# One multiplication per unit moved from VectorE to GpSimd, with a new order of work, in a fused recurrence and rational-activation kernel

## The chip, the cores and the metric

The kernel runs on one core of one Trainium2 chip. The metric is device time in microseconds (us). Before the change, three runs gave a median of 220.79 us, with 219.61 as the lowest and 221.04 as the highest.

A core has several engines that run side by side, each taking its own instructions strictly in order: PE (TensorE, matmuls), DVE (VectorE), ACT (ScalarE) and POOL (GpSimd). SP (SyncE) issues only DMAs here. POOL both computes and issues DMAs, and it can do that only in the order of its one queue.

## The reference

The first half is a gated linear recurrence over 768 positions, for 4 batches with 8 heads of 48 features. Its result, laid out as 3072 tokens of 384 features, goes into a two-layer block with a rational activation.

```python
f = 1.0 / (1.0 + np.exp(-f_logit))
for t in range(S):                       # S = 768
    state = f[:, :, t, :, None] * state + einsum('bhd,bhe->bhde', k[:, :, t], v[:, :, t])
    y[:, :, t] = einsum('bhd,bhde->bhe', q[:, :, t], state)

h = x @ w_in                             # 3072x384 @ 384x2048
P = a[0] + a[1]*h + a[2]*h**2 + a[3]*h**3
Q = 1.0 + abs(b[0])*abs(h) + abs(b[1])*h**2
out = (P / (Q + 1e-06)) @ w_out          # 3072x2048 @ 2048x384
```

## The kernel before

**Units.** The work is cut into 12 units. A unit is 256 positions of one batch, all heads at once; units 0 to 3 are the first 256 positions of the four batches, 4 to 7 the next, 8 to 11 the last. A unit's later batch-mate needs the state that the earlier one leaves.

**The recurrence part of a unit.** ACT makes the log of the forget gate (`ef`, `ls`, L190 and L195). PE sums it along positions with triangular matrices (`cs`, L205). ACT takes the exponential twice (`A n 0` and `A n 1`, L221): a decay factor for q and its inverse for k, each 128 partitions by 768 in float32. DVE multiplies the loaded q and k by them (`xa n 0` for q, `xa n 1` for k, L227), writing bf16. PE transposes both products (`T`, L239), and ACT copies the transposes out of PSUM (`Te`, L249). PE forms the scores (`sc`, L264); DVE masks them, reading PSUM (`mk`, two per unit, L272). PE adds up the output (`yi`, `yb`, L286), and ACT brings it to SBUF (`ye`, tile `xT`, L349). In between PE builds the new state (`kv`, `si`, tile `sv`), and DVE scales it, again reading PSUM (`st`, L359). GpSimd makes a small rearranged copy of v for each unit (`vm`, two per unit, L279).

**The block part of a unit.** PE multiplies `xT` by w_in, in four quarters of the hidden 2048 (`h`, tile `hp`, L368); ACT casts each quarter to bf16 (`hy`, L382). With this bf16 `hy`, DVE makes the square (`sq`, L386, tile `h`), the absolute value (`ab`, L394, tile `z`), and the numerator by steps `p1` (L428), `p2` (L433), `pm` (L442). Two sums of two tiles are needed, and each can be made in different ways:

- The denominator, square plus absolute value. PE can add both in PSUM by identity matmuls (`u`, L402, then `ln`, L407, as the logarithm on ACT). DVE can add them (`zv`, L412), or a DMA issued by POOL can accumulate (`zd`, L416); for these two, `lz` (L420) is the logarithm.
- The numerator's last sum, either by an accumulating DMA from POOL (`ta`, L446) or by DVE (`tv`, L450).

ACT then takes the exponential of the negative logarithm (`ex`, L424), DVE multiplies it on (`gm`, L454), and PE multiplies by w_out (`o`, L462). ACT copies the result out (`oe`, L469), and a DMA stores it.

**The order.** A string `ORDER` lists every step of all units. A loop at the end goes through it and issues each step; nothing is reordered afterwards, so the string sets the order on each engine and on each DMA queue. Numbers such as `8 16` are the sixteenths of the hidden dimension that a step covers, so `8 16` is one half of a unit and `4 8` a quarter. `@2` names one of four PSUM slots. `dz k` is k filler matmuls on PE. Loads of f, k and q are issued by SP, loads of v and of the weights by POOL. One piece of w_in is held back by a wait on the step `ls 1`, through a helper `behind` that makes an instruction wait until an earlier marked step has finished.

Of the kernel before, what the change touches and what calls it, by code (L numbers as in the profile page):

```python
# [29 lines left out]
def kernel(  # L30
# [12 lines left out]
    nc = tc.nc  # L43
# [3 lines left out]
    HP = H // 2  # L47
# [14 lines left out]
    ld = ctx.enter_context(tc.tile_pool(name="ld", bufs=3))  # L62
# [30 lines left out]
    marks = {}  # L93

    def unit(n):
        if n not in units:
            c, b = divmod(n, B)
            units[n] = dict(c=c, b=b, qk=qkp[n % 2], ls=lsp[n % 2], vm=vmp[n % 2], st=states[b])
        return units[n]

    def slot(i, shape, dtype, name):
        return slots[i].tile(shape, dtype, name=name, tag="s")
# [114 lines left out]
    def A(n, x, a0=0, a1=HP):  # L217
        s = unit(n)
        t = A_sb[:, :, x, 2 * D * a0:2 * D * a1]
        src = s["cs", a0][:, :, 0:2 * D * (a1 - a0)]  # L220
        nc.scalar.activation(t, src, AF.Exp, scale=1.0 if x else -1.0)  # L221

    def xa(n, x, *args):
        s = unit(n)
        a0, a1 = args or (0, HP)
        hh = slice(2 * a0, 2 * a1)
        return nc.vector.tensor_mul(  # L227
            s["qk"][:, :, x, hh, 0:D],
            s["qk"[x]][:, hh].rearrange("p h i d -> p i h d"),
            A_sb[:, :, x].rearrange("p i (h d) -> p i h d", h=H)[:, :, hh])  # L230

    def T(n, *args):
        s = unit(n)
        a0, a1, sl = args if len(args) == 3 else (0, HP, args[0])
        t = s["tp", a0] = slot(sl, [P, 2, 2, HP, P], BF16, "tp")
        for x in (1, 0):
            for i in range(2):
                for p in range(a0, a1):
                    nc.tensor.transpose(t[:, x, i, p, :],  # L239
                                        s["qk"][:, i, x, 2 * p:2 * p + 2, :].rearrange("t h d -> t (h d)"), ident)  # L240

    def Te(n, *args):
        a0, a1 = [x for x in args if x != "s"] or (0, HP)
        s = unit(n)
        if "T" not in s:
            s["T"] = at.tile([P, 2, 2, HP, P], BF16, name="qkT")
        d, t = s["T"][:, :, :, a0:a1], s["tp", a0][:, :, :, a0:a1]
        if "s" in args:
            return nc.scalar.copy(d.bitcast(F32).rearrange("p x i a t -> p (x i) (a t)"),  # L249
                                  t.bitcast(F32).rearrange("p x i a t -> p (x i) (a t)"))  # L250
        return nc.vector.tensor_copy(d.rearrange("p x i a t -> p (x i) (a t)"),
                                     t.rearrange("p x i a t -> p (x i) (a t)"))
# [224 lines left out]
    def behind(i, mark):  # L477
        tc.add_manual_dep(i.ins, marks[mark].ins.name,
                          mybir.DependencyInfo(mybir.DependencyClass.Sync, mybir.DependencyReason.DATA),
                          reason="begins behind it")  # L480

    steps = dict(ld=load, wi=load_w_in, wo=load_w_out, ab_=load_ab, cu=const_u, ci=const_i, cm=const_m,
                 cz=const_z, fa=coef_a, fb=coef_b, fr=coef_r, ef=ef, ls=ls, cs=cs, A=A, xa=xa, T=T, Te=Te,
                 sc=sc, mk=mk, vm=vm, yi=yi, yb=yb, kv=kv, si=si, ye=ye, ae=ae, st=st, h=h, hy=hy, sq=sq, ab=ab, u=u, ln=ln,
                 zv=zv, zd=zd, sa=sa, lz=lz, ex=ex, p1=p1, p2=p2, pm=pm, ta=ta, tv=tv, gm=gm, o=o, oe=oe, so=store, dz=dz)
    for step in ORDER.replace("\n", ";").split(";"):
        if step.strip():
            name, *args = step.split()
            marks[".".join([name] + [x for x in args if x.isdigit()])] = steps[name](
                *(int(x.lstrip("@")) if x.lstrip("@").isdigit() else x for x in args))  # L490


# [1 line left out]
_INS = ['q', 'k', 'v', 'f_logit', 'moe_w_in', 'moe_w_out', 'moe_a', 'moe_b']  # L494
_OUTS = [((3072, 384), 'float32')]


# [23 lines left out]
```

## Time and profile before

| | us |
|---|---|
| median of three runs | 220.79 |
| the profiled execution's own time | 220.24 |
| its span, first to last instruction | 218.4 |
| PE busy in the span | 204.7 |
| DVE busy in the span | 203.2 |
| ACT busy in the span | 199.9 |
| POOL busy in the span | 92.0 |

The span is 1.84 us shorter than the time of its execution; that remainder lies around the instructions. The busy time of PE contains modelled ends of overlapping matmuls, and a POOL instruction's busy time contains its stalls, so these two rows are rougher than those of DVE and ACT. The granted TensorE clock was at full speed for the whole span.

### The profile page before, as it was taken

How to read it: one execution, taken by the hardware profiler on the slowest of the kernel's cores; microseconds unless marked ns; L12 is line 12 of the kernel's file. 1: busy time of each engine (PE TensorE's matmuls, PEld its weight loads, DVE VectorE, ACT ScalarE, POOL GpSimd, SP SyncE). 2: the span in 40 equal slices, each digit the busy share in tenths (PEclk: the TensorE clock that was granted, in tenths of full speed). 3: DMA queues.
4: the chain of work that ended last, by engine and by line, in shares of the span. 5: the costliest groups of instructions: out<-in, count | busy, mean ns of one | idle time of the engine just before them, and what ended most of it. 6: DMA issues, size and time to landing. Idle time of an engine off the chain costs nothing.

```text
span 218.4 us, 7180 instructions
## 1 busy us (share of the span) xinstructions
PE 204.7 (94%) x3178; PEld 140.8 (64%) x3178; DVE 203.2 (93%) x247; ACT 199.9 (92%) x209; POOL 92.0 (42%) x91
## 2 busy tenths in 40 slices
PE   6999989889799999999999999999999999999992
PEld 2456758548477658657758658668668568686551
DVE  3577999999999999999999999999999999999991
ACT  4733999999999999999999999999999999999990
POOL 5250055969145901113953304954232526433300
PEclk9999999999999999999999999999999999999999
DMA  5999999999598999956999996999889794999853
GB/s 137 246 225 206 217 248 220 211 233 247 64 214 164 227 214 283 179 101 179 195 232 204 222 255 169 174 237 221 162 161 227 144 158 77 170 192 189 157 215 144
DMA packets 60911, 42.15 MB, mean 193 GB/s; under 512 B 51152, under 2 KB 54992, under 8 KB 60880
## 3 DMA queue, kind: packets, MB, share of 16 engines
q0 software_dynamic: 21232, 22.81, 65.4%
q1 hardware_dynamic: 39360, 18.68, 33.4%
q8 instruction: 25, 0.41, 0.8%
q10 hardware_dynamic: 288, 0.20, 0.3%
q14 instruction: 6, 0.05, 0.1%
HBM read 25.17 MB, written 4.72 MB: 137 GB/s over the span
## 4 chain that ended last, share of the span: by engine, by line
ACT 36%; DVE 31%; PE 21%; issue 5%; DMA 5%; SPq 0%; DVEq 0%; ACTq 0%
ACT qi L424 9%; ACT hy L382 9%; PE op L462 9%; PE hp L368 6%; ACT lq L420 5%; DVE scm L272 4%; DVE h L386 4%; DVE gall L454 4%; DVE qkp L227 4%; DVE gall L442 3%; DMA z<-h 3%; ACT A L221 3%; DVE gall L428 3%; DVE z L394 3%; DMA fn<-in_f_logit_dram 2%
## 5 line engine op out<-in xcount | busy, mean ns | idle before, releaser
L462 PE MATMUL op<-w_out_sb,gall 128*128 128x384 bf16 x384 | 70.1, 327 | 0.4 <-ACT hy L382 0.4
L368 PE MATMUL hp<-xT,w_in_sb 128*128 128x256 bf16 x576 | 66.6, 273 | 1.1 <-ACT xT L349 0.8
L368 PEld LDWEIGHTS <-w_in_sb 128*128 128x128 bf16 x576 | 56.0, 98 | 11.4 <-issue 2.8
L279 POOL COPY vmp<-vn 128x128 bf16<-128x128 bf16 x24 | 43.9, 1841 | 30.1 <-DMA vn<-in_v_dram 26.1
L462 PEld LDWEIGHTS <-gall 128*128 128x128 bf16 x384 | 35.4, 98 | 23.8 <-DVE gall L454 0.9
L382 ACT CAST hy<-hp 128x1024 bf16<-128x1024 f32 x48 | 47.2, 1068 | 2.3 <-PE hp L368 2.3
L424 ACT ACTIVATE qi<-lq 128x2048 bf16<-128x2048 f32 (+1 forms) x26 | 46.8, 1838 | 0.0
L420 ACT ACTIVATE lq<-z 128x2048 f32<-128x2048 bf16 (+1 forms) x20 | 36.9, 1847 | 0.6 <-DMA z<-h 0.6
L446 POOL DMA_DIRECT2D gall<-hy x17 | 14.8, 925 | 50.6 <-PE hp L368 18.4
L416 POOL DMA_DIRECT2D z<-h x18 | 17.6, 1081 | 30.3 <-issue 10.5
L454 DVE TENSOR_TENSOR gall<-gall,qi 128x2048 bf16<-128x2048 bf16 (+1 forms) x26 | 29.6, 1144 | 0.3 <-ACT qi L424 0.2
L442 DVE TENSOR_TENSOR gall<-gall,h 128x2048 bf16<-128x2048 bf16 (+1 forms) x26 | 29.4, 1143 | 0.0
L386 DVE TENSOR_TENSOR h<-hy 128x2048 bf16<-128x2048 bf16 (+1 forms) x26 | 27.4, 1063 | 2.1 <-ACT hy L382 2.1
L272 DVE TENSOR_TENSOR scm<-sc,mask 128x1024 bf16<-128x1024 f32 x24 | 28.4, 1218 | 0.0
L221 ACT ACTIVATE A<-cs 128x768 f32<-128x768 f32 (+1 forms) x26 | 19.5, 813 | 0.8 <-DVE qkp L227 0.8
L394 DVE TENSOR_SCALAR z<-hy 128x2048 uint16<-128x2048 uint16 (+1 forms) x28 | 17.4, 629 | 0.2 <-ACT hy L382 0.2
L428 DVE TENSOR_SCALAR gall<-hy,a_sb 128x4096 bf16<-128x4096 bf16 (+1 forms) x14 | 17.2, 1231 | 0.0
L433 DVE TENSOR_SCALAR hy<-hy,a_sb 128x4096 bf16<-128x4096 bf16 (+1 forms) x14 | 16.7, 1192 | 0.0
L114 POOL DMA_DIRECT2D vn<-in_v_dram x12 | 14.0, 1166 | 1.6 <-PE y L286 1.6
L349 ACT ACTIVATE xT<-y 128x768 bf16<-128x768 f32 x12 | 10.3, 858 | 4.1 <-PE y L286 4.1
L227 DVE TENSOR_TENSOR qkp<-kn,A 128x768 bf16<-128x768 f32 (+1 forms) x13 | 11.6, 893 | 2.1 <-ACT A L221 2.1
L239 PE MATMUL tp<-ident,qkp 128*128 128x128 bf16 x192 | 12.9, 219 | 0.2
(70 smaller groups left out, 262.1 us busy)
## 6 DMA issues: line engine op xcount, KB each, us to landing
gall<-hy POOLq DMA_DIRECT2D x16, 512.0 KB, 6.5
z<-h POOLq DMA_DIRECT2D x15, 512.0 KB, 7.3
fn<-in_f_logit_dram SPq DMA_DIRECT2D x11, 384.0 KB, 8.6
kn<-in_k_dram SPq DMA_DIRECT2D x11, 384.0 KB, 8.9
qn<-in_q_dram SPq DMA_DIRECT2D x11, 384.0 KB, 7.6
out_dram<-osb SPq DMA_DIRECT2D x11, 384.0 KB, 4.2
vn<-in_v_dram POOLq DMA_DIRECT2D x12, 192.0 KB, 7.7
w_in_sb<-in_moe_w_in_dram POOLq DMA_DIRECT2D x4, 384.0 KB, 9.9
```

What stands on the lines that cost most here:

```text
L221: nc.scalar.activation(t, src, AF.Exp, scale=1.0 if x else -1.0)
L272: return nc.vector.tensor_mul(t, s["sc", g].rearrange("s r a i t -> s (r a) (i t)"), mb)
L279: nc.gpsimd.tensor_copy(s["vm"][:, :, :, 32 * x:32 * x + 16], src)
L368: nc.tensor.matmul(t[:, m - m0, :], w_in_sb[:, kk, m * P:(m + 1) * P], s["x"][:, kk].rearrange("p i j t -> p (i j t)"), start=(kk == 0), s ...
L382: nc.scalar.copy(fl(big(s, "hy", "hy", 3), m0, m1), fl(s["hp", m0], 0, m1 - m0))
L386: return nc.vector.tensor_mul(fl(big(s, "h2", "h2", 2), m0, m1), fl(s["hy"], m0, m1), fl(s["hy"], m0, m1))
L394: return nc.vector.tensor_scalar(fl(big(s, "z", "z", 2), m0, m1).bitcast(U16), fl(s["hy"], m0, m1).bitcast(U16), 0x7FFF, None, op0=ALU.bit ...
L420: nc.scalar.activation(fl(lq, m0, m1), fl(s["z"], m0, m1), AF.Ln, scale=regs[2], bias=1.0 + 1e-6)
L424: nc.scalar.activation(fl(qi, m0, m1), fl(lq, m0, m1), AF.Exp, scale=-1.0)
L442: return nc.vector.tensor_mul(fl(s["g"], m0, m1), fl(s["g"], m0, m1), fl(s["h2"], m0, m1))
L454: return nc.vector.tensor_mul(fl(s["g"], m0, m1), fl(s["g"], m0, m1), fl(qi, m0, m1))
L462: nc.tensor.matmul(s["op"][:, j, 0:DM], s["g"][:, m, P * j:P * j + P], w_out_sb[:, m, :], start=(s["on", j] == 1), stop=(s["on", j] == KF))
```

## The change

Four things change in the code:

- `xa` takes a mark `p`. With it, the multiplication runs on GpSimd and not on VectorE, and it waits until the last "wide" step listed ahead of it has finished. Wide steps are `sq`, `ab`, `p1`, `p2`, `pm`, `gm`, `zv` and `tv`: DVE's steps on bf16 tiles in SBUF.
- From unit 3 to unit 11, the k product (`xa n 1`) carries this mark: nine of twelve. All q products stay on DVE.
- The ways of the two sums are drawn anew. Identity sums by PE (`u` with `ln`) go from 11 quarters to 2. DVE's `zv` goes from 2 halves to 6 halves and 4 quarters. DMA's `zd` goes from 15 halves and 3 quarters to 14 halves and 2 quarters, `ta` from 16 halves and 1 quarter to 17 halves and 2 quarters, and DVE's `tv` from 6 halves and 3 quarters to 5 halves and 2 quarters.
- `ORDER` is a new list. All other steps occur as often as before, with 39 filler matmuls where there were 38.

```diff
     def xa(n, x, *args):
         s = unit(n)
-        a0, a1 = args or (0, HP)
+        pool = "p" in args
+        a0, a1 = [y for y in args if y != "p"] or (0, HP)
         hh = slice(2 * a0, 2 * a1)
-        return nc.vector.tensor_mul(
+        i = (nc.gpsimd if pool else nc.vector).tensor_mul(
             s["qk"][:, :, x, hh, 0:D],
             s["qk"[x]][:, hh].rearrange("p h i d -> p i h d"),
             A_sb[:, :, x].rearrange("p i (h d) -> p i h d", h=H)[:, :, hh])
+        if pool:
+            behind(i, "wide")
+        return i
...
     for step in ORDER.replace("\n", ";").split(";"):
...
-            marks[".".join([name] + [x for x in args if x.isdigit()])] = steps[name](
+            i = marks[".".join([name] + [x for x in args if x.isdigit()])] = steps[name](
                 *(int(x.lstrip("@")) if x.lstrip("@").isdigit() else x for x in args))
+            if name in ("sq", "ab", "p1", "p2", "pm", "gm", "zv", "tv"):
+                marks["wide"] = i
```

Of the new order, these stretches matter below. DVE's steps around the nine GpSimd products are, by unit: the wide step that is waited for, and what DVE does next.

```
unit 3:  tv 0 8 16  | mk, st, mk, gm          unit 8:  p1 6 0 16 | mk, xa 8 0, st, mk, gm
unit 4:  p1 2 0 16  | mk, st, mk, gm          unit 9:  p1 7 0 16 | mk, st, xa 9 0, mk, p2
unit 5:  zv 3 0 8   | st, mk, mk, p1          unit 10: ab 8 8 16 | st, mk, mk, p1
unit 6:  gm 3 0 8   | mk, xa 6 0, mk, st, gm  unit 11: p1 9 0 16 | mk, mk, xa 11 0, gm
unit 7:  sq 5 0 8   | xa 7 0, mk, mk, st, gm
```

The start of the list, cut to the steps of units 0 and 1 that matter:

```
before: ld 0 f 2 4; ld 0 f 0 2; ld 1 f; ld 0 v; ld 0 k 0 2; ld 0 k 2 4; ld 0 q 2 4; ef 0 2 4; ls 0 2 4;
        ef 0 0 2; ls 0 0 2; ld 0 q 0 2; ef 1; ls 1; vm 0 1; wi 12 16 >ls.1; wi 8 12; wi 4 8; wi 0 4;
        A 1 0; T 0 2 4; ld 1 v; A 1 1; xa 1 1; ye 0; h 0 12 16; xa 1 0; h 0 8 12; T 1; h 0 4 8; h 0 0 4
after:  ld 0 v; ld 0 f 0 2; ld 0 q 0 2; ld 0 f 2 4; ld 0 k 0 2; ld 0 q 2 4; ef 0 0 2; ld 0 k 2 4; ls 0 0 2;
        A 0 0 0 2; ld 1 f; A 0 1 0 2; vm 0 1; ef 0 2 4; ls 0 2 4; wi 0 4; wi 8 12; wi 4 8; T 0 2 4; ef 1;
        ye 0; ls 1; h 0 0 4; A 1 0; h 0 8 12; A 1 1; h 0 4 8; wi 12 16 >ls.1; xa 1 1; ld 1 v; h 0 12 16;
        xa 1 0; T 1
```

2 lines of the change are left out of this document (1 added, 1 removed).

## The prediction

> **What bounds the kernel now.** The first view is the page's table of busy time with its chain of work that ended last.
>
> ```profile
> PE 204.7 (94%) x3178; PEld 140.8 (64%) x3178; DVE 203.2 (93%) x247; ACT 199.9 (92%) x209; POOL 92.0 (42%) x91
> ACT 36%; DVE 31%; PE 21%; issue 5%; DMA 5%; SPq 0%; DVEq 0%; ACTq 0%
> ```
>
> Three engines carry nearly the same load, and the chain changes over between them. So no single share names the bound; the stages must. The second view gives busy time in stretches: length, then PE, PEld, DVE, ACT, POOL.
>
> ```profile
> 0.00:20.00 20.00, 16.92 (x224) 8.68 (x225) 12.59 (x41) 8.97 (x15) 7.66 (x20) 1.00 1.09 203
> 60.00:80.00 20.00, 20.00 (x310) 13.64 (x308) 19.79 (x20) 20.00 (x22) 11.24 (x7) 1.00 0.99 203
> 180.00:200.00 20.00, 19.92 (x305) 15.10 (x303) 19.96 (x24) 19.96 (x19) 8.73 (x10) 1.00 0.82 155
> ```
>
> In the start ACT is idle for 20.00 - 8.97 = 11.0 us; later DVE and ACT have almost no idle time. The third view, the waits from 20 to 213 us, shows how little is left to gain there (us in total, times, longest):
>
> ```profile
> DVE h L386 <- ACT hy L382: 2.1, 3, 1.4
> DVE z L394 <- ACT hy L382: 0.2, 1, 0.2
> DVE gall L454 <- ACT qi L424: 0.2, 1, 0.2
> ACT hy L382 <- PE hp L368: 2.3, 3, 1.8
> ACT lq L420 <- DMA z<-h: 0.6, 2, 0.4
> ACT alast L355 <- PE sv L344: 0.3, 1, 0.3
> ```
>
> DVE waits 2.5 us in 193, ACT 3.2 us. An engine so full can end earlier only by having less to do or by starting earlier. Hence I ask for each engine how its work changes, and then whether the start moves.
>
> **The work of each engine.** Means of one instruction, from the groups by shape:
>
> ```profile
> L227 DVE TENSOR_TENSOR qkp<-kn,A 128x768 bf16<-128x768 f32 x11 | 10.5, 954 | 0.0
> L412 DVE TENSOR_TENSOR z<-z,h 128x2048 bf16<-128x2048 bf16 x2 | 2.4, 1222 | 0.0
> L450 DVE TENSOR_TENSOR gall<-gall,hy 128x1024 bf16<-128x1024 bf16 x3 | 2.1, 691 | 0.0
> L420 ACT ACTIVATE lq<-z 128x2048 f32<-128x2048 bf16 x17 | 33.7, 1980 | 0.6 <-DMA z<-h 0.6
> L420 ACT ACTIVATE lq<-z 128x1024 f32<-128x1024 bf16 x3 | 3.3, 1093 | 0.0
> L407 ACT ACTIVATE lq<-u 128x1024 f32<-128x1024 f32 x11 | 11.2, 1039 | 0.0
> ...
> 158.79 1.21 DVE L272 TENSOR_TENSOR scm<-sc,mask 128x1024 bf16<-128x1024 f32 x1
> 159.93 0.55 DVE L359 TENSOR_TENSOR state<-sv,alast 128x384 bf16<-128x384 f32 x1
> 160.39 1.21 DVE L442 TENSOR_TENSOR gall<-gall,h 128x2048 bf16<-128x2048 bf16 x1
> ...
> 46.91 1.83 PE u L402 x8
> ```
>
> In the timeline rows a step starts 0.08 us before its predecessor ends (158.79 + 1.21 is 160.00, the next starts at 159.93), so a DVE step takes its mean less 0.08: `mk` 1.14, `st` 0.46.
>
> - DVE. Nine k products go: 9 x 0.87 = 7.8 us less. Added: 4 halves of `zv`, 4 x 1.14, and 4 quarters, 4 x 0.61 (the size of the 691 ns row); dropped: one half and one quarter of `tv`, 1.14 + 0.61. Together 4.6 + 2.4 - 1.75 = 5.25 more. Net 2.6 us less.
> - ACT. Nine logarithms of quarters from PSUM go, 9 x 1.039 = 9.35; three halves and three quarters from SBUF come, 3 x 1.980 + 3 x 1.093 = 9.22. Net 0.1 us less: ACT keeps its load.
> - PE. Nine `u` steps of four matmuls go. The chain row gives 1.83 / 8 = 0.229 each: 36 x 0.229 = 8.2 us less, one filler more, so 8.0 less.
> - POOL issues as many accumulating DMAs as before (35 against 35), plus nine products.
>
> Since ACT is as full as DVE and loses nothing, I cost the relief of DVE and PE at 0 on the path. It is cover for what follows.
>
> **The product on GpSimd and the wait.** The trace has no such product, only copies on POOL, and they tell much.
>
> ```profile
> 0.31 0.10 POOL L505 MEMSET const-float32-0.0<- 128x1 f32 x1 [0.31 <-issue]
> 44.12 0.30 POOL L279 COPY vmp<-vn 128x128 bf16<-128x128 bf16 x1
> 134.91 5.42 POOL L279 COPY vmp<-vn 128x128 bf16<-128x128 bf16 x1
> 142.64 0.53 POOL L279 COPY vmp<-vn 128x128 bf16<-128x128 bf16 x2
> 182.92 0.58 POOL L279 COPY vmp<-vn 128x128 bf16<-128x128 bf16 x1
> ...
> 134.34 0.96 DVE L227 TENSOR_TENSOR qkp<-qn,A 128x768 bf16<-128x768 f32 x1
> ...
> 138.95 1.23 DVE L386 TENSOR_TENSOR h<-hy 128x2048 bf16<-128x2048 bf16 x1
> 140.24 0.56 DVE L359 TENSOR_TENSOR state<-sv,alast 128x384 bf16<-128x384 f32 x1
> ...
> 183.17 0.89 DVE L394 TENSOR_SCALAR z<-hy 128x2048 uint16<-128x2048 uint16 x1
> ```
>
> The same copy takes 0.27 us (0.53 for two) or 5.42. The long one began at 134.91, while DVE ran steps on SBUF tiles without a gap, and ended at 140.33, just when `st`, which reads PSUM, had begun. So DVE's SBUF steps keep POOL out, and its PSUM steps let it in. The hold uses that: the product starts when the wide step has ended and DVE does `mk`, `st`, `mk`, which last 1.14 + 0.46 + 1.14 = 2.74 us.
>
> How long is the product? Below: 0.10 fixed plus 0.20 per 128 elements (the 0.30 us row less the memset), six times, 1.3 us. Above: twice the 0.20, if the two inputs are read in turn, 2.5 us. I take 1.6, six times the 0.27 row, and 0.1 to start. [...]
>
> Does a product that has started hold up DVE? At 182.92 a copy ran for 0.58 us, and the `ab` at 183.17 took 0.89 us where 0.69 is usual (the row at 185.11 below): some 0.2 us lost, about one copy.
>
> ```profile
> 185.11 0.68 DVE L394 TENSOR_SCALAR z<-hy 128x2048 uint16<-128x2048 uint16 x1
> ```
>
> I take it that DVE's next SBUF step waits to the product's end. For units 3, 4, 5 and 10 the window is 2.74 us: nothing lost. Unit 7's `xa 7 0` starts first and the product uses the window behind it: nothing. Unit 11 has 2.28: nothing. Unit 9 has 1.60: 0.1. Units 6 and 8 have one `mk`, 1.14: 0.6 each. Sum 1.3 us; with 1.3 us a product 0.6, with 2.5 us 4.2 (1.5 + 1.5 + 1.0 + 0.3, rounded). So DVE's net is -1.3, between -2.0 and +1.6. Only the last would show past ACT. [...]
>
> Behind the waiting product in POOL's queue stand `vm` copies, loads of v and the accumulating DMAs; mostly these need DVE steps that come after the window, so I cost the queue at nothing. If a `vm` copy ahead is shut out, the product is late too: a rival below.
>
> **The start.**
>
> ```profile
> 4.40 0.52 ACT L190 ACTIVATE fn<-fn 128x384 f32<-128x384 f32 x1 [2.31 <-DMA fn<-in_f_logit_dram]
> 7.86 0.84 ACT L195 ACTIVATE lsp<-fn 128x768 bf16<-128x768 f32 x1
> 5.37 0.98 SPq L114 DMA_DIRECT2D qn<-in_q_dram  x2
> 11.19 1.12 DVE L227 TENSOR_TENSOR qkp<-qn,A 128x384 bf16<-128x384 f32 x2 [0.69 <-DMA qn<-in_q_dram]
> 18.04 0.81 ACT L349 ACTIVATE xT<-y 128x768 bf16<-128x768 f32 x1 [4.12 <-PE y L286]
> 19.10 2.79 PE hp L368 x24
> DMA to landing us min/median/max: 7.1/9.9/12.8
> ```
>
> Before, the last q product of unit 0 waits for its load, issued at 5.37, and ends at 12.31. After, q is issued second and fifth. ACT then goes from 4.40 through two gates, two logarithms and four half factors, about 8 x 0.45 us, with some 1.9 us for prefix sums and the register loads: 9.9, and the product ends near 10.5, 1.8 us earlier. Fewer fillers stand ahead of the transposes, so I put `xT` of unit 0 at 15.9 in place of 18.04: 2.1 us earlier. But what ran in that idle time now comes behind it: on ACT `ls 1`, `A 1 0` and `A 1 1` (about 0.7 each, 2.1 us), on DVE both products and one state step of unit 1 (2 x 0.87 + 0.46 = 2.2). Gain and debt cancel: 0, between -2.1 (the moved steps fall into the waits that `h` and `hy` leave) and +3 (below).
>
> **Sum.** On the profiled execution's 220.24: ACT -0.1, start 0, DVE and PE 0 behind ACT; 220.1. The median of the runs lies 0.55 above that execution, so 220.7. A measurement of this kernel can hardly tell less than 1% (2.2 us) from no change.
>
> **Rivals.**
>
> 1. The start's gain stays. ACT waits 2.3 us for `hp` in the third view, and if the moved steps fill such holes, the 2.1 us are kept: 218.6. For it: ACT's 11.0 idle us at the start are by far its largest. Against: the fillers in the new list mark holes that stay. Chance 0.20, half of it beyond 1%; should a third of ACT's 3.2 us of waits go too, it is 217.5.
> 2. Slower: the window is missed. If the factor on ACT, the load of k or a `vm` copy ahead is more than about 1.1 us late against the wide step (2.74 less 1.6), the product meets DVE's run of SBUF steps and is shut out as the copy was: 5.42 - 0.27 = 5.2 us. `T`, `Te`, `sc` and the next `mk` stand behind it. I take half as covered by queued steps, and two of nine units: 2 x 2.6 = 5.2, less DVE's 1.3: 224.6. Unit 11 is the likeliest, as its factor is issued beside the first `mk`. For it: POOL's `vm` copies already wait so. Against: the waited-for steps sit ahead of long windows in six of nine. Chance 0.27.
> 3. The last piece of w_in. It waits for `ls 1`, which ended at 8.7 us before and now follows `xT`: 15.9 + 0.8 + 0.7 is 17.4. It is issued by 18.1, and landing takes 7.1 (the quickest of the four before) to 9.9, so 25.2 to 28.0. PE wants it for `h 0 12 16`, ahead of `T 1`: 16.7, plus three quarters of `h` at 2.79 / 2, 4.2, plus prefix sum, state and one `u`, 1.75, plus 8 fillers, 1.8, is 24.4. A stall of 0.8 to 3.6, 2 taken: 222.7. It decides once the landing is later than 24.4. Chance 0.15.
> 4. The product doesn't run beside PSUM steps but on DVE's time, 2.5 us each: DVE +1.6, 221.9 to 222.3. This is in the forecast's width.
>
> **How the numbers follow.** The forecast, 220.7 within 219.3 to 222.3, has 0.38; rivals 1 to 3 have 0.20, 0.27 and 0.15. Faster by over 1% (under 218.6): half of rival 1 and a little of the forecast's own error, 0.15. Slower by over 1% (over 223.0): rival 2 and a part of 3, 0.33. Within 1%: 0.52. The range leaves a tenth on each side: 217.5 to 225.5, the top holding rival 2 with a third window missed in part.
>
> **What would show it.** Right: nine products on POOL of 1.3 to 2.5 us that begin within 0.2 us after the wide step; DVE busy 2 to 3 us lower, with idle time; ACT's busy time within 0.5 us of 199.9; `u` in two steps; `xT` of unit 0 near 16. Wrong: products of 4 to 6 us, waits of PE's `tp` for POOL, SBUF steps of DVE drawn out by over a microsecond, ACT idle in the middle, or `hp` waiting for w_in near 25 us.

## The result and the profile after

| | before | after |
|---|---|---|
| median of six runs, us | 220.42 | 230.63 |
| lowest and highest | 219.61 to 221.25 | 228.43 to 232.31 |
| the profiled execution's own time | 220.24 | 230.92 |
| its span | 218.4 | 229.2 |

The kernel after takes 1.0431 times as long as the kernel before (95% interval 1.0373 to 1.0489); this ratio and its interval leave out runs that took over 1.5% longer than the fastest, here two of the six, while the median is over all six. The prediction said 220.7 within 217.5 to 225.5; the kernel is 10 us slower than before.

The page of the kernel after: busy times, TensorE's granted clock in 40 slices, and the shares of the chain that ended last.

```profile
PE 204.5 (89%) x3143; PEld 140.8 (61%) x3143; DVE 205.3 (90%) x244; ACT 201.2 (88%) x206; POOL 84.2 (37%) x100
PEclk9999997976999999999999999999999997999999
PE 37%; DVE 29%; ACT 19%; issue 9%; DMA 3%; POOL 1%; ACTq 0%; POOLq 0%; DVEq 0%
```

PE leads the chain with 37%, where it had 21%, and "issue", time in which an engine waits for nothing that the profile shows, went from 5% to 9%. The clock row has 7s and a 6 where the kernel before has only 9s. ACT's busy time is nearly what it was. So the 10 us are idle time of ACT. To see where, here is the busy time in three stretches (columns as in the prediction; the fourth busy time is ACT's), first of the kernel before, then of the kernel after.

```profile
0.00:68.00 68.00, 60.90 (x961) 40.44 (x962) 58.91 (x94) 55.71 (x69) 31.98 (x38) 1.00 1.14 206
68.00:180.00 112.00, 109.57 (x1834) 77.53 (x1833) 111.17 (x112) 111.04 (x111) 48.86 (x43) 1.00 1.00 195
180.00:218.40 38.40, 34.25 (x388) 22.86 (x385) 33.07 (x43) 33.18 (x32) 11.16 (x12) 1.00 0.74 163
```

```profile
0.00:68.00 68.00, 57.24 (x865) 36.93 (x866) 54.58 (x89) 51.28 (x61) 25.31 (x39) 0.92 1.15 211
68.00:180.00 112.00, 105.60 (x1778) 76.39 (x1777) 111.53 (x109) 109.32 (x111) 48.46 (x51) 1.00 0.94 178
180.00:229.20 49.20, 41.65 (x504) 27.44 (x501) 39.17 (x48) 40.65 (x36) 10.46 (x11) 0.97 0.73 160
```

The length of a stretch less ACT's busy time is ACT's idle time. It sums up with the busy time to the span:

| ACT, us | before | after | difference |
|---|---|---|---|
| idle, 0 to 68 | 12.3 | 16.7 | 4.4 |
| idle, 68 to 180 | 1.0 | 2.7 | 1.7 |
| idle, 180 to the end | 5.2 | 8.5 | 3.3 |
| busy | 199.9 | 201.2 | 1.3 |
| span | 218.4 | 229.2 | 10.8 |

So the loss has three places. Each is read below from the kernel after.

**The middle: products that meet.** The groups of GpSimd's product and of the q product on DVE (busy us, then mean ns of one), and two pieces of the timeline, of unit 6:

```profile
L228 POOL TENSOR_TENSOR qkp<-kn,A 128x768 bf16<-128x768 f32 x9 | 17.1, 1901 | 13.7 <-ACT A L221 13.6
L228 DVE TENSOR_TENSOR qkp<-qn,A 128x768 bf16<-128x768 f32 x11 | 13.9, 1261 | 0.0
...
97.78 2.06 POOL L228 TENSOR_TENSOR qkp<-kn,A 128x768 bf16<-128x768 f32 x1
...
98.09 2.58 DVE L228 TENSOR_TENSOR qkp<-qn,A 128x768 bf16<-128x768 f32 x1
```

The nine products take 1.81 to 2.15 us; none is as long as the copy of 5.42 us in the kernel before. But `xa 6 0` began 0.3 us after the product and took 2.58 us in place of 0.95. It ended at 100.67, 0.8 us after the product's end at 99.84, so nearly its own length behind it. Two others are drawn out, those of units 8 and 9; they end at 134.84 and 151.66, again 0.8 us after their products (134.02 and 150.84):

```profile
132.70 2.14 DVE L228 TENSOR_TENSOR qkp<-qn,A 128x768 bf16<-128x768 f32 x1
150.39 1.27 DVE L228 TENSOR_TENSOR qkp<-qn,A 128x768 bf16<-128x768 f32 x1
```

Above 0.95 these are 1.63 + 1.19 + 0.32 = 3.1 us.

**Beginning and end: TensorE's clock.** In its span, the trace of the kernel after has half clock from 34.98 us for 3.41 us, from 48.63 for 6.83, twice that, and from 188.58 for 3.41. So here is busy time in stretches of 3.4 us, around the 7s of the clock row (the first busy time is PE's; the third number from the end is the granted clock, the next the DMA engines' share):

```profile
31.50:34.90 3.40, 1.94 (x78) 1.27 (x78) 3.34 (x5) 3.37 (x5) 1.30 (x4) 1.00 0.94 219
34.90:38.40 3.50, 3.46 (x43) 2.22 (x43) 3.50 (x5) 3.50 (x6) 3.08 (x4) 0.51 1.02 142
45.20:48.60 3.40, 1.45 (x36) 0.86 (x36) 3.40 (x4) 3.40 (x5) 1.06 (x1) 1.00 1.25 202
48.60:52.00 3.40, 2.45 (x77) 1.48 (x77) 3.40 (x5) 3.40 (x4) 0.76 (x1) 0.51 1.21 266
52.00:55.40 3.40, 2.86 (x14) 2.00 (x14) 3.40 (x5) 2.39 (x3) 1.53 (x1) 0.50 1.19 256
181.70:185.10 3.40, 2.71 (x123) 2.03 (x120) 3.40 (x4) 3.40 (x3) 0.05 (x1) 1.00 1.08 208
185.10:188.50 3.40, 1.40 (x20) 1.02 (x21) 3.40 (x4) 1.92 (x4) 0.87 (x1) 1.00 0.52 98
188.50:191.90 3.40, 3.40 (x19) 2.46 (x17) 0.35 (x1) 1.78 (x2) 0.85 (x1) 0.51 0.99 198
```

In four stretches the clock is 0.5, and ahead of each stands one in which PE was busy for little: 1.94, 1.45, 2.45 (itself at half clock) and 1.40 of 3.4 us. In the kernel before, cut in the same way, the least busy stretch around this time has 2.37, and the next keeps the full clock:

```profile
40.10:43.50 3.40, 2.37 (x61) 1.45 (x49) 3.40 (x6) 3.40 (x6) 3.40 (x3) 1.00 1.24 211
43.50:46.90 3.40, 2.76 (x85) 1.48 (x84) 3.40 (x5) 3.40 (x4) 1.59 (x3) 1.00 1.18 242
```

Busy time alone doesn't draw the line. In the kernel after, the stretch from 99.80 to 103.20 has 1.89 us and the clock stays full, and in the kernel before, cut at other points, those of 3.4 us from 42.10 and from 55.80 have 1.99 and 2.00, with the same outcome. Another count separates better: the columns that the matmuls starting in a stretch move, weighted by the size that their rows show: `128*128` as 1, `64*64` as a quarter, and so on. Over the 1008 stretches of full clock in all seventeen traces, laid on the moments at which the clock changes, each of the 20 with under 2530 such columns was followed by half clock, none of the 961 with over 3160, and 8 of the 27 between; by busy time, halved and unhalved ones mix from 1.56 to 2.64 us. This is a count from the matmul records, of which some can be missing, and no run was built to test it.

Why PE is less busy there, the rows of the identity sums show (first and last start), in the kernel before and in the kernel after, from 20 to 60 us:

```profile
L402 PE MATMUL u<-h,ident x20: 376/379/390, 22.6 to 59.3; 128*128 128x512 bf16 x20
```

```profile
L406 PE MATMUL u<-h,ident x4: 376/378/379, 25.3 to 29.1; 128*128 128x512 bf16 x4
```

Each comes with as many on tile `z`. Of the 36 matmuls that the change takes off PE, 32 stood between 20 and 60 us, and that is where the clock falls. They are of size `128*128` and move 512 columns, so each adds 512 to the count above. That their absence opens the idle time, and not the new order around them, is argued from this: no run puts them back.

**The end: a pause.** The timeline of PE:

```profile
184.01 0.41 PE L337 MATMUL sv<-vn,qkp 64*64 64x48 bf16 x28
187.10 0.22 PE L337 MATMUL sv<-vn,qkp 64*64 64x48 bf16 x4 [2.69 <-issue]
```

PE stops for 2.69 us inside `kv 11`, four matmuls before its last, and waits for nothing that the profile shows. The halved clock from 188.5 follows from it here. It need not: in the run below with the load of v behind the constants, a pause of 2.83 us falls across two stretches (1.88 and 2.10 us busy), and the clock stays full.

### The profile page after: what moved, and what is told of

It is laid out like the page before. It is cut to its first block, busy times and chain, and to the rows that moved or that the text cites. A ratio compares the mean times of both kernels' runs of the same rounds, so it can differ in the third digit from the quotient of the medians.

```text
span 229.2 us, 7115 instructions
## 1 busy us (share of the span) xinstructions
PE 204.5 (89%) x3143; PEld 140.8 (61%) x3143; DVE 205.3 (90%) x244; ACT 201.2 (88%) x206; POOL 84.2 (37%) x100
## 4 chain that ended last, share of the span: by engine, by line
PE 37%; DVE 29%; ACT 19%; issue 9%; DMA 3%; POOL 1%; ACTq 0%; POOLq 0%; DVEq 0%
PE op L466 13%; PE hp L372 12%; DVE h L390 4%; ACT lq L424 4%; DVE gall L458 4%; DVE scm L276 4%; ACT hy L386 4%; DVE gall L446 4%; DMA w_in_sb<-in_moe_w_in_dram 3%; PE warm L214 3%; ACT qi L428 3%; DVE gall L432 3%; DVE qkp L228 2%; PE y L290 2%; PE cs L205 2%
## 5 line engine op out<-in xcount | busy, mean ns | idle before, releaser
L372 PE MATMUL hp<-xT,w_in_sb 128*128 128x256 bf16 x576 | 70.7, 282 | 4.4 <-ACT xT L353 3.1
L372 PEld LDWEIGHTS <-w_in_sb 128*128 128x128 bf16 x576 | 57.7, 101 | 16.5 <-issue 5.6
L424 ACT ACTIVATE lq<-z 128x2048 f32<-128x2048 bf16 (+1 forms) x26 | 45.2, 1743 | 0.0
L450 POOL DMA_DIRECT2D gall<-hy x19 | 17.0, 927 | 46.8 <-DVE gall L446 31.9
L283 POOL COPY vmp<-vn 128x128 bf16<-128x128 bf16 x24 | 18.1, 846 | 23.6 <-DMA vn<-in_v_dram 17.5
L228 POOL TENSOR_TENSOR qkp<-kn,A 128x768 bf16<-128x768 f32 x9 | 17.1, 1901 | 13.7 <-ACT A L221 13.6
L228 DVE TENSOR_TENSOR qkp<-qn,A 128x768 bf16<-128x768 f32 (+1 forms) x13 | 15.0, 1153 | 2.9 <-ACT A L221 2.9
L290 PE MATMUL y<-scm,vn 64*32 64x128 bf16 x384 | 13.2, 231 | 4.6 <-DVE scm L276 4.6
L114 POOL DMA_DIRECT2D vn<-in_v_dram x12 | 13.5, 1127 | 6.7 <-PE sv L348 4.1
```

What stands on the lines that cost most here:

```text
L228: i = (nc.gpsimd if pool else nc.vector).tensor_mul(s["qk"][:, :, x, hh, 0:D], s["qk"[x]][:, hh].rearrange("p h i d -> p i h d"), A_sb[:, ...
L372: nc.tensor.matmul(t[:, m - m0, :], w_in_sb[:, kk, m * P:(m + 1) * P], s["x"][:, kk].rearrange("p i j t -> p (i j t)"), start=(kk == 0), s ...
L424: nc.scalar.activation(fl(lq, m0, m1), fl(s["z"], m0, m1), AF.Ln, scale=regs[2], bias=1.0 + 1e-6)
```

## The experiments

A ratio is always to the kernel before, run on the same chip beside it. Where a kernel has more filler matmuls than the kernel after, their results are read by nobody, and the output stays the reference's.

### Undoing one thing at a time

**All products on DVE.** The nine marks `p` go:

```diff
-xa 3 1 p; ... xa 11 1 p;
+xa 3 1; ... xa 11 1;
```

> The changed kernel with all nine k products back on VectorE; its order and its sums stay. Theory A (the products are a gain that other things outweigh): VectorE has 9 x 0.87 = 7.8 us more to do and loses the 3.1 us by which products now draw out the q products of units 6, 8 and 9; it is full from 60 to 180 us, so the time rises by 2 to 5 us, to 232.5 to 235.5. Theory B (GpSimd's products beside VectorE are the loss): the time falls by 3 us or more, to 227 or below.

235.14 us (ratio 1.0666, 1.0614 to 1.0718). The product on GpSimd isn't what costs: in this order it gains 4.5 us. The order with its sums alone costs about 14 us.

**The load of v behind the constants.** In the kernel after, POOL issues `ld 0 v` ahead of the triangular matrices, so the first matmuls start later; they wait for the matrices for 3.4 us, where the kernel before has 1.8:

```diff
-ab_ b a; cz 2; cz 0; cz 1; cz 3; ld 0 v; ld 0 f 0 2; ... cu 1; ld 0 k 0 2; ci;
+ab_ b a; cz 2; cz 0; cz 1; cz 3; ld 0 f 0 2; ... cu 1; ci; ld 0 v; ld 0 k 0 2;
```

> The changed kernel with the load of v of unit 0 behind the constants on GpSimd's queue, as it was before the change. Theory A: the first fillers on TensorE start near 1.8 us and not at 3.4, the first prefix sum near 5.5 and not at 7.5, the first xT near 16 and not at 17.8; the time falls by 1 to 2 us, if the later v load does not hold the weights up. Rival (a late start is made up later, or the weights' loads set the pace): within 0.5 us of the changed kernel.

230.65 us (1.0428, 1.0369 to 1.0487). `xT` of unit 0 comes 0.9 us earlier (16.91 for 17.79) and that of unit 1 1.0 (35.1 for 36.08), but the median is that of the kernel after. Alone it isn't measurable. Single traces differ by as much: in the five runs that leave the order up to this point as it is, `xT` of unit 0 starts between 17.79 and 19.61.

**No hold on the last piece of w_in.**

```diff
-wi 12 16 >ls.1;
+wi 12 16;
```

> The changed kernel without the hold of the last piece of w_in behind the logarithm of unit 1. Theory A: that piece is issued near 12 us and not at 19.6, the matmuls of unit 0's last quarter no longer wait from 24.8 to 27.6, xT of unit 1 comes 2 to 3 us earlier than at 36.1, and the time falls by 1 to 3 us. Rival (the piece then takes the other loads' bandwidth): xT of unit 1 moves by less than 1 us, the time by less than 0.7 us.

231.49 us (1.0455, 1.0383 to 1.0527). In the kernel after, PE waits for that piece for 0.88 us at 27.59, as the prediction's third rival had it; here that wait is gone, yet `xT` of unit 1 starts at 36.16 as before. The piece isn't on the path.

**The q products out of the windows.** `xa 6 0`, `xa 8 0` and `xa 9 0` move behind the second `mk`, so that they don't meet the product:

```diff
-xa 6 0; o 2 1 4 8; mk 5 1; so 0 0 2 s; vm 6 1; st 5 0; xa 6 1 p;
+o 2 1 4 8; mk 5 1; so 0 0 2 s; vm 6 1; st 5 0; xa 6 0; xa 6 1 p;
```

> The changed kernel with VectorE's q products of units 6, 8 and 9 moved behind both masking steps, so that the GpSimd product meets only steps that read PSUM. Theory A: these three q products take 0.95 us and not 2.58, 2.14 and 1.27, and the time falls by 2 to 3 us. Rival (VectorE is not what holds units 6 to 9 up): the q products are short again, the time moves by less than 1 us.

228.44 us (1.0365, 1.0309 to 1.0421). All q products take 0.95 us again and DVE is busy for 202.2 us, 3.1 less. The median is 2.2 us lower, but the intervals of the two ratios overlap. The traces bear the gain out: `xT` of unit 9 follows that of unit 3 after 95.90 us here and after 98.29 in the kernel after, 2.4 less.

**The sums of unit 9 off the DMA engines.**

```diff
-zd 9 0 8; ... zd 9 8 16;
+zv 9 0 8; ... zv 9 8 16;
```

> Edit: the two sums z of unit 9, accumulated by DMA in the kernel after (2 x 512 KB around 170 to 184 us, where the DMA engines are full), become two additions on VectorE of about 1.0 us each. Theory A (the pause of 2.7 us in kv of unit 11 is an instruction fetch that stands behind the data in the DMA engines): the pause goes or falls under 1 us, with it the halved clock at 188 to 192; minus 4.3 us plus up to 2 us of VectorE: 228 to 229. Rival B (the pause has another cause): it stays at 2.3 to 3.2 us; median 230.6 to 232.6.

230.39 us (1.0427, 1.0376 to 1.0478): no gain in time, but the pause is gone. The stretches of this kernel around it:

```profile
180.00:182.00 2.00, 0.60 (x18) 0.44 (x18) 2.00 (x3) 2.00 (x2) 0.00 (x0) 1.00 0.89 170
182.00:184.00 2.00, 2.00 (x20) 0.86 (x18) 2.00 (x3) 2.00 (x2) 1.26 (x1) 0.63 0.04 8
184.00:186.00 2.00, 2.00 (x15) 0.89 (x8) 2.00 (x3) 0.25 (x1) 0.55 (x1) 0.51 0.00 0
186.00:188.00 2.00, 2.00 (x90) 1.51 (x89) 2.00 (x2) 0.45 (x1) 0.00 (x0) 1.00 0.00 0
```

The DMA engines are idle from 182 to 188 us, and `kv 11` runs through. In exchange DVE, with two additions more, gives the state late (PE waits 1.81 us for it), and `xT` of unit 10 starts at 187.55 in place of 183.31; PE is busy for 0.60 of 2 us, and the clock halves all the same. One loss took the place of the other.

**The beginning of before.** The order up to `ye 0 s` is that of the kernel before, with w_in in the sequence of the kernel after; then follows the order of the kernel after.

> Edit: the beginning of the order up to xT of unit 0 is that of the kernel before (with the pieces of w_in in the sequence in which the kernel after reads them); from there on the order of the kernel after. Theory A (about 3 us of the loss are made in the beginning, before xT of unit 1): xT of unit 1 at 33 to 34 us instead of 36.1, and the median 2 to 3 us lower, 227.6 to 228.6. Rival B (the beginning is not what counts, since what follows catches up or waits for something else): xT of unit 1 at 35 to 37, median 230 to 231.

229.83 us (1.0381, 1.0335 to 1.0428). `xT` of unit 1 comes at 34.99, 1.1 us earlier and not 2 to 3; the median is 0.8 lower, inside the uncertainty. Theory A had the size wrong by more than half, and the result lies at the edge of rival B's.

**Unit 1's transposes early, too.** On top of that, `xa 1 0`, `T 1` and `Te 1` go among the first pieces of `h` of unit 0:

```diff
-h 0 0 4 @0; hy 0 0 4; ... hy 0 8 12; ... u 0 8 12 @2; ... xa 1 0; ... T 1 @2; ... Te 1 s;
+h 0 0 4 @0; xa 1 0; hy 0 0 4; ... T 1 @2; hy 0 8 12; ... Te 1 s; u 0 8 12 @2;
```

> Edit: the run with the beginning of the kernel before, and beside it the transposes of unit 1 and their copy on ScalarE put where the kernel before has them, among the first pieces of h of unit 0, ahead of its u. Theory A (what is left of the loss between xT of unit 0 and xT of unit 1 is that ScalarE takes the copy of unit 1's transposes only at 31 us, behind all of unit 0's casts, instead of 22.8 us): xT of unit 1 at 32.5 to 33.5 us instead of 35.0, and the median 1 to 2 us lower, 228 to 229. Rival B (ScalarE's work in sum sets xT of unit 1, whatever its sequence): xT of unit 1 at 34.5 or later, median 229.5 to 231.

233.98 us (1.0592, 1.0537 to 1.0646); `xT` of unit 1 at 39.49, 4.5 us later. The transposes now stop PE for 2.05 us, and the clock halves from 24.9 to 28.3 us; its mean over the span is 0.963, for 0.97 in the run above. That is worse than either theory allowed. Whether the late copy on ACT sets unit 1 stays open, because this edit adds a stop of its own.

### Filling PE's idle time

```diff
+    def dv(n, k):
+        t = unit(n)["svt"]
+        for i in range(k):
+            nc.tensor.matmul(t[:, 1, 384:512], Ui, Ui, start=False, stop=True, skip_group_check=True)
...
-yb 1 2 4 @1; ... yi 1 1; yb 1 0 2; ... cs 3 @1; ... sc 2 1 @3; ... si 2 1; ... ye 2 s;
+dz 5 @1; yb 1 2 4 @1; ... yi 1 1; dz 5 @0; yb 1 0 2; ... dz 4 @0; cs 3 @1; ... sc 2 1 @3; dv 2 24; ... dv 2 24; si 2 1; ... ye 2 s; dv 2 24;
```

> Edit: idle TensorE stretches ahead of the first two half-clock windows (31.5 to 34.9 us, TensorE busy 1.94 of 3.4; 45.2 to 48.6 us, busy 1.45 of 3.4) are filled with 172 matmuls whose results nobody reads. Theory A (TensorE's clock is halved for a window of 3.4 us after a window in which it was little busy): no 0.50 between 30 and 56 us, and the start of xT of unit 4 some 1.8 us earlier, 84.8 instead of 86.6; the median 1.5 to 2 us lower, about 228.8. Rival B (the halving is tied to something else, or the fillers only push the chain back): the halved windows stay, or xT of unit 4 stays within 0.5 us of 86.6 or comes later; median 230.5 to 233. On the pause of TensorE in kv of unit 11 (2.7 us): if it belongs to a place in the instruction stream, it comes 172 matmuls and weight loads earlier in the program, ahead of kv 11; if it belongs to the work that stands there (kv 11 or the full DMA queue around it), it stays in kv 11.

(The edit adds 86 matmuls and as many weight loads, so 172 instructions; the expectation calls them all matmuls.) 229.74 us (1.0443, 1.04 to 1.0486). No stretch has a clock of 0.5 any more (0.998 in the mean of the span, for 0.97 in the kernel after), and the pause left `kv 11`; it now stands in `sc 11`, with 0.79 us. But the median is only 0.9 lower, since the fillers ahead of `yb 1` wait 1.60 us for a buffer and push `xT` of unit 1 from 36.08 to 37.94. Theory A is right about the clock. `xT` of unit 4, which it wanted 1.8 us earlier, comes 1.3 later (87.91 for 86.63), as rival B had it, and the median lies between the two.

**Four edits at once**: v behind the constants, no hold on w_in, q products out of the windows, and these fillers.

> Edit: four edits on the kernel after at once: the load of v of unit 0 behind the constants, no hold on the last piece of w_in, the q products of units 6, 8 and 9 behind both mk, and the 86 filling matmuls (with as many weight loads) of the run before. Theory A (the losses are separate and add up): from 230.6 minus 0.5 to 1 for the load of v, 0 for w_in, 2.2 for the windows, 0.9 for the fillers with the clock and the pause: 226.5 to 227.5. Rival B (the losses hide one another, the slack is used up elsewhere): 228.5 or more, no lower than the windows alone.

225.19 us (1.0233, 1.0209 to 1.0256): 5.4 us off, more than the sum of the single runs and more than either theory expected.

**The same with better places**: the ten fillers at unit 1 also go into the spare columns of `sv` (6 ahead of `yb 1 2 4` and 4 ahead of `yb 1 0 2`), again 86 in all.

> Edit: the run with four edits at once, but with the ten filling matmuls at y of unit 1 written beside the sums of the state (6 and 4, of 128 columns) instead of into a buffer of their own, for which TensorE waited 1.6 us; 86 fillers as before, so that the instruction stream has the same length. Theory A (of the 4.9 us that are left, 1.6 to 2 come from that buffer): xT of unit 1 at 34 to 34.6 us instead of 36.1, median 223 to 224. Rival B (what is gained at unit 1 is lost again further on, since ScalarE's work sets the pace from there, or the clock falls again without the longer fillers): median 224.7 to 226.

222.91 us (1.0148, 1.0103 to 1.0194), `xT` of unit 1 at 33.80. Of the 10 us, 7.7 are gone. Its three stretches:

```profile
0.00:68.00 68.00, 60.65 (x999) 40.98 (x1001) 56.78 (x91) 53.69 (x63) 23.85 (x39) 1.00 1.20 217
68.00:180.00 112.00, 108.84 (x1884) 78.88 (x1883) 110.43 (x111) 111.14 (x112) 51.46 (x51) 1.00 0.95 182
180.00:220.80 40.80, 35.56 (x349) 23.25 (x346) 34.77 (x44) 35.58 (x33) 8.70 (x10) 0.99 0.77 171
```

ACT's idle time is 14.3, 0.9 and 5.2 us: middle and end are those of the kernel before, and what is left, 2.0 us, lies in the first 68 us. To the median of the kernel before, 220.0 in these runs, 2.9 us are left. They weren't taken apart further.

**The same without fillers.**

> Edit: the load of v of unit 0 behind the constants, no hold on the last piece of w_in, the q products of units 6, 8 and 9 behind both mk, and no fillers. Against the run with the same three and the fillers it measures what the halved clock and the pause in kv of unit 11 cost together. Theory A (they cost the 3 to 4 us that the trace of after shows between xT of units 10 and 11, and 1 to 2 around 50 us): halved windows and a pause over 2 us in kv of unit 11, median 227.5 to 229. Rival B (the fillers did nothing, the windows did it): 225 to 226.

227.86 us (1.0327, 1.0283 to 1.0372). The halved stretches are back (mean clock 0.962, for 0.998 with fillers), and the pause stands in `kv 11` with 3.17 us. So the fillers alone bring 227.86 - 222.91 = 4.95 us: halved clock and pause together. The two profiled executions differ by more, 6.3 us of span, and show where: `xT` of unit 10 starts 2.2 us later here (180.68 for 178.44), and that of unit 11 follows it after 16.26 us here and after 12.26 with fillers, another 4.0. The larger part thus lies at the pause and the half clock behind it, the smaller at the half clock of the beginning.

**The same with fillers, and the k products on DVE.**

> Edit: as the run beside it with the fillers moved, and the nine k products on VectorE in their places instead of on GpSimd. It measures the product where the other losses are mended; in the order of after it was worth 4.5 us. Theory A (VectorE's 0.87 us each set the pace in this order): 4 to 5 us slower than the run beside it, 227.5 to 228.5. Rival B (ScalarE sets the pace, which is busy 90% of the span in each kernel): within 1.5 us of the run beside it.

229.33 us (1.043, 1.0385 to 1.0475). The product on GpSimd is worth 6.4 us in the mended order, near the 9 x 0.87 = 7.8 us that it takes off DVE. Both sizes expected were too small. This order leaves DVE no room.

**Fillers and windows with the beginning of before and unit 1's transposes early**, 94 fillers in all:

> Edit: the kernel with the beginning of before and unit 1's transposes early, the q products of units 6, 8 and 9 behind both mk, and 94 filling matmuls at places where TensorE is idle (not ahead of a buffer). Theory A (the sum of the terms read from the traces: beginning 2 to 3, windows 2.2, halved clock and pause 4 to 5): no 0.50 in the clock, no pause in kv of unit 11, q products of 0.95 us, and 230.6 minus 8 to 9: 221.5 to 223. Rival B (the new order itself is slower by more than these terms): the traces show all of these mended, and the time is still 225 or more.

227.8 us (1.0347, 1.0292 to 1.0402). Full clock (0.999 in the mean), q products of 0.95 us, no pause in `kv 11` itself, and yet 4.9 us more than with the beginning of the kernel after: the early transposes cost here too. `xT` of unit 1 comes at 36.92 and not at 33.80, and a pause of 1.85 us stands ahead of `sc 11`, where the other run has 0.57. As a test of the sum it failed by that choice.

### The product in the order of before

```diff
-xa 3 1; ... xa 11 1;
+xa 3 1 p; ... xa 11 1 p;
```

The order and the splits of the kernel before, and only the nine products on GpSimd.

> Edit: the order and the splits of the kernel before, with nothing changed but the k products of units 3 to 11, which go to GpSimd behind the preceding wide step, as in the kernel after. It measures the product by itself. Theory A (the product is a small gain or nothing, the loss sits in the new order): nine products of 0.87 us leave VectorE, each takes 1.8 to 2.1 us on GpSimd and draws out what VectorE does beside it by up to 1 us; within 2 us of the kernel before, 219 to 223. Rival B (the product on GpSimd itself costs, because this order was found with the products on VectorE): GpSimd's copies and DMA issues queue behind held products, VectorE or TensorE waits for them; 225 or more.

233.5 us (1.061, 1.0572 to 1.0647). Rival B: the same edit that gains 4.5 to 6.4 us in the new order loses 13.3 here. PE's waits in this kernel (us in total, times, longest):

```profile
PE sv L337 <- POOL qkp L228: 6.9, 3, 2.7
PE tp L243 <- POOL qkp L228: 3.2, 4, 1.4
```

**The products early.** Each is listed right behind its decay factor, and the factor of k ahead of that of q:

```diff
-A 4 1; A 4 0; ... xa 4 0; ... xa 4 1;
+A 4 1; xa 4 1 p; ... A 4 0; ... xa 4 0;
```

> Edit: the order of the kernel before, with the nine k products on GpSimd and each of them listed right behind its decay factor, which ScalarE makes ahead of that of q. It tells whether the 13 us that the product cost in the order of before come of its late place. Theory A (the product is late for the transposes and for kv; with more room it costs nothing): the waits of TensorE for GpSimd's product, 10.1 us in the run with the products in their old places, fall under 3 us, and the time is 220 to 224. Rival B (the order of before has no room for a product of 1.8 us on GpSimd: earlier products hold up GpSimd's copies and DMA issues, or ScalarE's decay factors come out of turn): 227 or more.

229.3 us (1.0417, 1.0395 to 1.0438). The waits for the product fall to 1.7 us, and 9 us of loss remain. The page and a product of this kernel beside DVE's steps:

```profile
PE 205.6 (91%) x3171; PEld 141.3 (62%) x3178; DVE 209.8 (92%) x238; ACT 201.0 (89%) x209; POOL 93.3 (41%) x100
...
102.56 5.67 POOL L228 TENSOR_TENSOR qkp<-kn,A 128x768 bf16<-128x768 f32 x1 [5.86 <-ACT A L221]
...
106.83 1.96 DVE L398 TENSOR_SCALAR z<-hy 128x2048 uint16<-128x2048 uint16 x1 [0.26 <-ACT hy L386]
108.71 1.31 DVE L390 TENSOR_TENSOR h<-hy 128x2048 bf16<-128x2048 bf16 x1
```

Without a window this product takes 5.67 us, the others 1.80 to 2.67; the `ab` at 106.83 takes 1.96 where 0.7 is usual. DVE has nine products of 0.87 us less than the kernel before and is still busy for 209.8 us, not 203.2 - 7.8 = 195.4: the 14 us between are steps drawn out like that `ab`, up to a `sq` and a `pm` of 3.08 us where 1.21 is usual.

### Where the pause stands

Some of these kernels have more PE instructions ahead of the pause than the kernel after. The following rows of PE's timeline show it in the run with the beginning of before (2 filler matmuls more), in the run with four edits and the better places (86 more), and in the run with both, beginning and 94 fillers (96 more):

```profile
186.39 0.24 PE L337 MATMUL sv<-vn,qkp 64*64 64x48 bf16 x6 [2.89 <-issue]
```

```profile
184.21 0.41 PE L273 MATMUL sc<-qkT 48*64 48x128 bf16 x15 [0.57 <-issue]
```

```profile
187.63 1.16 PE L377 MATMUL hp<-xT,w_in_sb 128*128 128x256 bf16 x9 [1.85 <-issue]
```

With 2 more, it comes 2 matmuls earlier in `kv 11` (6 left, not 4). With 86 more it stands behind the first matmul of `sc 11`, and with 10 more than that, 10 matmuls ahead (9 of `h 10` left and that one). So it goes with a place in PE's instruction stream. From the place in `kv 11` to that in `sc 11` are 42 matmuls of the kernel (4 and 8 of `kv`, 1 of `si`, 4 of `o`, 24 of `h`, 1 of `sc`); with the 86 added, 128, each with its weight load: 256 instructions. The load on the DMA engines matters beside the place: in the kernel after, their share is 1.08 from 181.7 to 185.1 us and the pause 2.69; in the run without the sums of unit 9 on them, it is 0.04 and 0.00 from 182 to 188 us, and there is no pause.

The traces also show DMA queues of the kind that the page calls `instruction`. One of them, in the kernel after:

```profile
q8 instruction: 24, 0.39, 0.7%
```

These are 24 packets of 16384 bytes. In the kernel after one of them runs from 184.83 to 185.73 us, inside the pause from 184.41 to 187.10. In all twelve traces with such a pause, in `kv 11`, `h 10` or `sc 11`, a packet ends in the pause or up to 0.8 us ahead of it, and PE goes on 1.26 to 1.55 us after the packet's end. Where the packet comes early enough there is no pause: in the run without those DMAs it ends at 183.71, and PE reaches the place in `kv 11` only at 188.6. That PE waits here for its instructions is argued from these times and from the name of the queue; that the packet is late because it stands behind the accumulating DMAs, from the DMA shares and that one run. No row shows what PE or the packet waits for.

## Why the prediction was wrong

**"I cost the relief of DVE and PE at 0 on the path. It is cover for what follows."** This is the step that failed, for PE. The 8.0 us of identity sums were taken as work that hides behind ACT and can go without effect. In the new kernel PE idled between 31 and 49 us, its clock was halved for 10 us between 35 and 55 us, and near the end it paused for 2.69 us, with half clock behind that. The two together cost 4.95 us, by the runs with and without fillers, and by their traces the end has the larger part. The sum had no term for either. That filling PE's idle time restores the clock is shown (0.998 in the mean, for 0.97); that the identity sums were what had kept it up is likely but not tested by itself. The pause is another matter than the sums' work: it goes with the place in the instruction stream and, as argued above, with the load on the DMA engines there. The prediction looked at neither PE's work in stretches of 3.4 us nor the clock behind them, although its first view gave PE 94% of the span.

**DVE, net -1.3.** The mechanism was right, the size wrong. The q product beside a GpSimd product ends 0.8 us after it, in units 6, 8 and 9 alike, so it waits to its end, as predicted, and no further step is touched. But the product takes 1.9 us in the mean, where 1.6 was taken, and the three windows cost 3.1 us and not 1.3. With the windows mended, DVE's busy time is 202.2, 1.0 less than before, where -2.6 stood. And DVE is not behind ACT in this order: 2.4 of the 3.1 us show in the progress of units 3 to 9, and the nine products are worth 4.5 to 6.4 us of time, where their relief stood at 0.

**ACT, -0.1.** Its busy time rose by 1.3 us, and its idle time by 9.5. The step "ACT keeps its load" was near, but it said nothing of whether ACT could be fed.

**The start, 0 between -2.1 and +3.** It came out past the upper end: ACT has 4.4 us more idle time up to 68 us, part of it from the clock (the fillers bring `xT` of unit 3 from 69.08 to 66.82). `xT` of unit 0 was to come at 15.9 and came at 17.79:

```profile
1.34 1.05 POOL L114 DMA_DIRECT2D vn<-in_v_dram  x1 [0.82 <-POOLq L511]
...
17.79 0.81 ACT L353 ACTIVATE xT<-y 128x768 bf16<-128x768 f32 x1 [3.68 <-PE y L290]
```

The prediction followed SP's queue and not POOL's, on which `ld 0 v` now stands ahead of the constants. With v behind them and w_in free it is at 16.09, and at 15.91 with the fillers too. That the moved work cancels this gain held: alone, the edit with v changed no median.

**Rival 2, the missed window,** was seen in no product of the kernel after. It exists: the run with products early in the order of before has one of 5.67 us, close to the 5.4 of the copy on which the price was based. **Rival 3** has the landing right (27.59, within 25.2 to 28.0) and the stall of 0.88, but it costs nothing, as the run without the hold shows. **Rival 1** is refuted by `xT` of unit 1, 3.5 us later than before.

**"The queue at nothing"** is contradicted by no run in the new order, and it would be wrong elsewhere: in the order of before the same nine products cost 13.3 us, with PE waiting 10.1 us in all for them.

## What to carry to other kernels

Before work is taken off TensorE, look at how busy it stays in each 3.4 us, not in the span: here stretches with 1.40 to 1.94 us of work were followed by half clock, and 86 matmuls whose results nobody reads brought 5 us back, the larger part of it by moving a pause of TensorE, which took 0.57 us at its new place and not 3.17. The nine multiplications on GpSimd were worth 6.4 us, of the 7.8 that they take off VectorE, where they lie beside steps that read PSUM; early in the order of before, mostly without such windows, VectorE was busy for 6.6 us more with them than without. When an order is drawn anew, edit and order are best priced apart: here the edit gains 4.5 to 6.4 us and the order loses 14.

## What was not expected of the hardware

- The clock halved after a stretch of 3.4 us in which TensorE was busy for 1.94 us, so far from idle; after another with 1.89 us it didn't. The columns moved, weighted as above, tell the two apart better (2144 and 2944).
- In eight runs TensorE paused 2.3 to 3.2 us for no releaser at one place in its instruction stream, with a DMA share of 1.08 ahead of it in the kernel after, until 1.3 to 1.6 us after a packet of 16384 bytes on the instruction queue. In the three runs with 86 matmuls added the pause stood 256 instructions further on and took 0.56 to 0.79 us.
- A GpSimd product of 128 x 768 elements takes 1.81 to 2.15 us in its window in the kernel after, and 1.80 to 5.67 in the run with the products early.
